# 52 matmuls of a constant by itself, at the start of an FFT and mixture-of-experts kernel

## The chip, the cores and the metric

The kernel runs on one core of one Trainium2 chip. The metric is device time in microseconds of one execution. Six names come up for the engines: PE is TensorE (matmuls), PEld its weight loads, DVE is VectorE, ACT is ScalarE, POOL is GpSimd and SP is SyncE, which issues most of the DMAs here.

## What is computed

The real part of a two-dimensional Fourier transform of each of 8 batches of 2496 x 256, and then a mixture of 8 experts with one expert for each of the 19968 rows:

```python
def _attn_ref(x):                       # x: 8 x 2496 x 256, f32
    X = np.fft.fft(x, axis=1)
    X = np.fft.fft(X, axis=2)
    return X.real.astype(np.float32)

def _moe_ref(x, modality_id, w_gate, modality_bias, w1, w2):
    logits = x @ w_gate + modality_bias[modality_id]
    e_idx = np.argmax(logits, axis=1)
    ...                                 # gate_w: softmax weight of the chosen expert
    for e in range(E):                  # 8 experts, 256 -> 1024 -> 256
        mask = e_idx == e
        h = np.maximum(x[mask] @ w1[e], 0.0)
        out[mask] = gate_w[mask, None] * (h @ w2[e])
    return out
```

## The kernel before

The transform is done batch by batch as small matrix products. Stage 1 (line 540) multiplies x by constants `c1`: for each of two halves of the 10 column groups of a batch (`c` = 0 and 1) there are four units, each with its own PSUM tile of the pool `psf`, which has four slots, and ACT copies each unit out of PSUM (line 513). In the first batches the products are in f32. For the scale of the numbers ACT also squares the input and sums it up (line 394), four times for a batch, and four small matmuls by `ones` (line 418) add the sums over the partitions. Stages 2 and 3 (lines 571 and 586) follow, then a routing step that puts each row on the list of its expert (GpSimd scatters the rows to DRAM), and blocks of 256 rows that run through the two products of their expert (lines 1099 and 1119). These blocks take most of PE's time, and the transform of later batches runs between them.

The expert weights arrive in f32 and are split into two f16 parts each. `wload` (line 827) loads 1024 KB into a tile `wa`; `wfold` (lines 835 and 836) adds and subtracts its two halves on DVE; `wnorm` (line 849) takes the norm by matmuls of the weights by themselves into a tile of the PSUM pool `psm`, which has three slots; then follow the split (lines 870 and 877) and the store to DRAM.

At the beginning SP issues the loads in this order: a part of x, half of `c1`, further parts of x, the other half of `c1`, the packed constants and small tables. Then `ones` is set by a memset on DVE (line 293). All DMAs of SP go down one queue.

The order of the instructions on each engine is not that of the program: the framework plans it with modelled times (`schedule_with_timeline_sim=True`, line 1313), by what is ready and by place in the program, and each engine then runs its list in that order. Where the kernel says `issue_after` or `high_priority`, it bends that plan.

Of the kernel before, what the change touches and what calls it, by code (L numbers as in the profile page):

```python
# [13 lines left out]
F32 = mybir.dt.float32  # L14
# [8 lines left out]
P = 128  # L23
# [48 lines left out]
ORDER0 = "rrrrrrrfssssFssss"  # L72
PACK = 1000 + 512
UB = 3
RV = 1
FG = 6
ORDER_S = (0, 1, 2), (0, 1, 2, 3, 3, 4, 4, 5, 5, 6, 6, 7, 7), (5, 6, 7, 0, 1, 2, 3, 4)
# [121 lines left out]
class Group:  # L199


    def __init__(self, k, b, g0, rp, tail, dsti):
        self.k, self.b, self.g0, self.gn = k, b, g0, min(CH, G - g0)
        self.rp, self.tail, self.dsti, self.list, self.first = rp, tail, dsti, None, False
# [28 lines left out]
class Pads:  # L233

    b, list = B - 1, None
# [8 lines left out]
class Kernel:  # L244
    def __init__(self, ctx, tc, t):
        self.ctx, self.tc, self.nc, self.t = ctx, tc, tc.nc, t
        nc = self.nc
        pool = lambda name, bufs=1, **k: ctx.enter_context(tc.tile_pool(name=name, bufs=bufs, **k))
        self.cpool = c = pool("consts")
        self.fft = pool("fft", 2)  # L250
        self.rt = pool("route", 2)
        self.psf = pool("psf", 4, space=PSUM)
        self.psm = pool("psm", 3, space=PSUM)
        self.pso = pool("pso", 1, space=PSUM)
        self.pool = pool

        self.ready = -1
        self.early = True
        self.head = None
        self.XM = [None, None]  # L260

        def const(name, shape, dt=F32):
            x = c.tile(shape, dt, name=name)
            nc.sync.dma_start(x, t["c_" + name])
            return x

        self.load_x(0, 0, 0)
        self.c1 = c.tile([P, NI, 132], F32, name="c1")
        nc.sync.dma_start(self.c1[:, 0:NH], t["c_c1"][:, 0:NH])
        self.load_x(0, 0, 1)  # L270
        if XE:
            self.load_x(0, 1, 0)
            nc.sync.dma_start(self.c1[:, NH:NI], t["c_c1"][:, NH:NI])
            self.load_x(0, 1, 1)
            pk = const("pack", [P, PACK])
        else:
            pk = const("pack", [P, PACK])
            self.load_x(0, 1, 0)
            nc.sync.dma_start(self.c1[:, NH:NI], t["c_c1"][:, NH:NI])
            self.load_x(0, 1, 1)  # L280
        self.mp = pk[:, 0:512].rearrange("p (a c) -> p a c", a=4)
        self.misc = pk[:, 512:584]
        self.pk = pk
        self.wg = pk[:, 584:616].rearrange("p (a c) -> p a c", a=4)
        self.e3 = pk[0:120, 616:616 + 2 * P].rearrange("p (a c) -> p a c", a=2)
        self.iota = pk[0:1, 872:1000]
        self.ids = const("ids", [P, B, NC], I32)
        self.tri = const("tri", [P, 2, P], F16)
        self.mb = c.tile([P, 2, 8], F32, name="mb")
        nc.sync.dma_start(self.mb, t["mb"].unsqueeze(0).to_broadcast([P, 2, 8]))  # L290

        self.ones = c.tile([P, P], BF16, name="ones")
        nc.vector.memset(self.ones, 1.0)
        self.base = c.tile([P, 8], F32, name="base")
        nc.vector.tensor_copy(self.base, self.misc[:, 16:24])
        pad = c.tile([P, ROW], I16, name="padrow")
        nc.gpsimd.memset(pad, 0)
        padi = pad.bitcast(I32)
        nc.gpsimd.memset(padi[:, 256:257], OOB)
        self.padrow = pad  # L300
        for i in range(2):
            self.scatter_dep(nc.sync.dma_start(t["xd"][DUMP + i * P: DUMP + (i + 1) * P, :], pad), 0)
        self.done = c.tile([1, 8], F32, name="done0")
        nc.vector.memset(self.done, 0.0)
        self.ntok = 0
        self.extra = 0
        self.ntaken = 0
        self.nblk = 0
        self.loads = []
        self.pend = []  # L310
        self.rows = None
        self.nslot = NSLOT
        self.prev = None
        self.ob = None
        self.off = 0
        self.mark = None
        self.bases = {}
        self.pos = 0.0
        self.paced = None, 0, 1
        self.slots = lambda b: 1  # L320
        self.hold = ()
# [65 lines left out]
    def fold_add(self, b, c):  # L387
        n = 4 if b < UB else 2
        if c == 0:
            self.sq = self.fft.tile([P, n], F32, name=f"nst{n}")  # L390
        if b < UB:
            jk = self.wp.tile([P, NH * D], F16, name="xj", bufs=1)
            for h in range(2):
                self.nc.scalar.activation(jk.rearrange("p (i d) -> p i d", i=NH), self.XM[c][:, h], AF.Square, accum_out=self.sq[:, 2 * c + h:2 * c + h + 1])
            return
        X = self.XM[c][:, 0]
        for i0, i1 in PARTS:
            self.nc.vector.tensor_tensor(X[:, i0:i1], X[:, i0:i1], self.XM[c][:, 1, i0:i1], ALU.add)
        self.nc.scalar.activation(self.XM[c][:, 1], X, AF.Square, accum_out=self.sq[:, c:c + 1])
# [56 lines left out]
    def scale(self, b):  # L456
# [6 lines left out]
        inv = rt.tile([P, 1], F32, name="xinv")  # L463
        self.pow2(self.total(self.sq, self.psf.tile([P, 512], F32, name="psf")), eb, s, 204 if b >= FB else 188, 2.0 if b < UB else 1.0)
        V.tensor_scalar(inv.bitcast(I32), eb.bitcast(I32), float(66 << 23), None, ALU.add)
# [7 lines left out]
    def fold(self, b, c):  # L473
# [7 lines left out]
        elif c == 0:  # L481
            self.fold_add(b, 0)
            self.fold_add(b, 1)
            self.scale(b)
        if b < UB:
            self.PQ = self.XM[c][:, :, :, 0:P], self.XM[c][:, :, :, P:D]
# [33 lines left out]
    def stage1(self, b, c):  # L520
# [3 lines left out]
        for h, src in enumerate(self.PQ):  # L524
# [3 lines left out]
            for i0, n in ((0, 3), (3, 2)):  # L528
# [4 lines left out]
                for i in range(n):  # L533
                    o = v[:, :, 12 * i:12 * i + 12]
                    if b >= FB:
                        for k, (a, w) in enumerate(HL):
                            nc.tensor.matmul(o, src[:, a, i0 + i, :], self.c1h[:, w, i1 + i, :], start=k == 0, stop=k == 2)  # L537
                    elif b < UB:
                        for k in range(2):
# [5 lines left out]
                else:  # L545
                    self.copy(T1[:, :, cols], v, b < UB and (h + i0 // 3) % 2 < E1)
                yield
# [775 lines left out]
```

## Time and profile before

| | us |
|---|---|
| median of three timed runs | 1032.98 |
| lowest and highest of them | 1031.93, 1036.22 |
| the profiled execution | 1029.87 |
| its span, first to last instruction | 1028.0 |
| PE busy in the span | 999.3 |
| DVE, ACT, POOL busy | 542.7, 443.3, 368.7 |

The profile is of one execution, and its rows give the time from the span's start. Matmuls are pipelined: one begins before the one ahead of it has ended, so the distance of two starts is the price of one, and the duration is longer. The idle time of an engine is put down to what released it. A row of the timeline in which equal instructions are merged gives the first start, the time from there to the last end, and how many there are.

### The profile page before, as it was taken

How to read it: one execution, taken by the hardware profiler on the slowest of the kernel's cores; microseconds unless marked ns; L12 is line 12 of the kernel's file. 1: busy time of each engine (PE TensorE's matmuls, PEld its weight loads, DVE VectorE, ACT ScalarE, POOL GpSimd, SP SyncE). 2: the span in 40 equal slices, each digit the busy share in tenths (PEclk: the TensorE clock that was granted, in tenths of full speed). 3: DMA queues.
4: the chain of work that ended last, by engine and by line, in shares of the span. 5: the costliest groups of instructions: out<-in, count | busy, mean ns of one | idle time of the engine just before them, and what ended most of it. 6: DMA issues, size and time to landing. Idle time of an engine off the chain costs nothing.

```text
span 1028.0 us, 25873 instructions
## 1 busy us (share of the span) xinstructions
PE 999.3 (97%) x9910; PEld 904.1 (88%) x9910; DVE 542.7 (53%) x1607; ACT 443.3 (43%) x870; POOL 368.7 (36%) x351
## 2 busy tenths in 40 slices
PE   7999899999999999999999999999999999999996
PEld 6878789898998899999999998888888888899996
DVE  2869767586866558779763347423232322222221
ACT  4775676466643354455533333233332323233332
POOL 0077822136414432735343334345451212121111
PEclk9999999999999999999999999999999999999999
DMA  9847969268459858988766963887788895594991
GB/s 335 328 140 234 368 165 302 73 229 255 153 153 283 310 172 240 300 258 281 229 188 199 232 184 86 268 258 238 173 241 229 259 256 176 159 289 139 235 205 36
DMA packets 149725, 227.65 MB, mean 221 GB/s; under 512 B 116309, under 2 KB 117375, under 8 KB 132695
## 3 DMA queue, kind: packets, MB, share of 16 engines
q1 hardware_dynamic: 133031, 183.75, 61.8%
q0 software_dynamic: 16560, 42.15, 11.5%
q8 instruction: 80, 1.31, 0.5%
q14 instruction: 54, 0.44, 0.1%
HBM read 191.77 MB, written 62.48 MB: 247 GB/s over the span
## 4 chain that ended last, share of the span: by engine, by line
PE 77%; issue 10%; DMA 7%; POOL 2%; DVE 2%; ACT 1%; POOLq 0%; SPq 0%; ACTq 0%
PE psm L1099 33%; PE pso L1119 33%; DMA wa<-w 4%; DMA XM<-x 2%; PE psf L540 2%; PE psf L566 2%; POOL out L1128 2%; PE psf L584 2%; PE psf L571 2%; PE psf L537 2%; PE psf L586 1%; DMA c<-c_c 0%; PE psm L849 0%; ACT w L870 0%; DMA xT<-xd 0%
## 5 line engine op out<-in xcount | busy, mean ns | idle before, releaser
L1099 PE MATMUL psm<-xT,w 128*128 128x256 f16 (+1 forms) x4368 | 453.3, 260 | 5.4 <-DVE H L1105 3.3
L1119 PE MATMUL pso<-w,H 128*128 128x256 f16 x3864 | 450.5, 273 | 2.7 <-ACT ob L1127 2.7
L1099 PEld LDWEIGHTS <-w 128*128 128x128 f16 x4368 | 383.6, 98 | 44.3 <-issue 4.3
L1119 PEld LDWEIGHTS <-H 128*128 128x128 f16 x3864 | 375.2, 98 | 45.5 <-issue 3.2
L1105 DVE SCALAR_TENSOR_TENSOR H<-psm,H 128x512 f16<-128x512 f32 x322 | 219.9, 687 | 331.9 <-ACT H L1104 331.2
L1128 POOL DMA_INDIRECT out<-ob,ig x161 | 163.6, 1016 | 514.1 <-ACT ob L1127 484.0
L1104 ACT ACTIVATE H<-psm 128x512 f16<-128x512 f32 x322 | 190.7, 596 | 224.3 <-PE psm L1099 223.1
L1127 ACT ACTIVATE ob<-pso,gs 128x256 f32<-128x256 f32 x161 | 68.6, 471 | 247.6 <-PE pso L1119 204.5
L709 POOL DMA_INDIRECT xd<-rp,dsti x88 | 102.1, 1161 | 96.4 <-DVE rm L228 49.2
L709 POOL DMA_INDIRECT xd<-rm,dsti x88 | 94.3, 1072 | 35.5 <-issue 18.3
L518 DVE SCALAR_TENSOR_TENSOR T<-psf,T 120x280 f16<-120x280 f32 (+2 forms) x95 | 43.2, 462 | 42.3 <-ACT T L517 42.2
L877 DVE SCALAR_TENSOR_TENSOR w<-wa,wsc,w 128x512 f16<-128x512 f32 (+1 forms) x52 | 42.5, 867 | 10.8 <-ACT w L870 10.8
L517 ACT ACTIVATE T<-psf 120x280 f16<-120x280 f32 (+2 forms) x95 | 38.7, 421 | 10.2 <-PE psf L537 5.7
L571 PE MATMUL psf<-m2u,T 128*120 128x280 f32 x132 | 37.2, 403 | 1.8 <-DVE Lg L594 1.0
L540 PE MATMUL psf<-c,XM 128*128 128x132 f32 x240 | 31.9, 296 | 6.8 <-DMA c<-c_c 6.8
L540 PEld LDWEIGHTS psf<-c,XM 128*128 128x128 f32 x240 | 30.8, 206 | 7.0 <-DMA XM<-x 6.7
L584 PE MATMUL psf<-T,pack 120*128 120x145 f16 x330 | 34.7, 224 | 1.4 <-DVE T L518 1.4
L870 ACT ACTIVATE w<-wa,wsc 128x1024 f16<-128x1024 f32 (+1 forms) x24 | 33.4, 1426 | 4.3 <-DVE wsc L406 3.5
L566 PE MATMUL psf<-pack,T 128*120 128x144 f16 (+1 forms) x330 | 31.3, 229 | 0.0
L513 ACT COPY T<-psf 120x280 f32<-120x280 f32 (+2 forms) x57 | 22.7, 407 | 16.6 <-PE psf L571 7.3
L856 ACT ACTIVATE xj<-wa 128x1024 f16<-128x1024 f32 x20 | 21.1, 1054 | 18.2 <-DMA wa<-w 7.4
L517 ACT ACTIVATE rp<-psf 128x256 f16<-128x256 f32 x55 | 21.0, 383 | 16.2 <-PE psf L584 12.5
(186 smaller groups left out, 596.9 us busy)
## 6 DMA issues: line engine op xcount, KB each, us to landing
w<-w SPq DMA_DIRECT2D x80, 1028.0 KB
w<-w SPq DMA_DIRECT2D x80, 1024.0 KB
XM<-x SPq DMA_DIRECT2D x14, 1280.0 KB
wa<-w SPq DMA_DIRECT2D x16, 1024.0 KB
out<-ob,ig POOLq DMA_INDIRECT x161
XM<-x SPq DMA_DIRECT2D x2, 768.0 KB
xT<-xd SPq DMA_TRANSPOSE x91
xd<-rp,dsti POOLq DMA_INDIRECT x88
```

The lines of the kernel that those rows point to most:

```text
L517: self.acted = self.nc.scalar.activation(dst[:, 0], ps, AF.Identity, scale=scale).ins
L540: self.staged = nc.tensor.matmul(o, src[:, k, i0 + i, :], self.c1[:, i1 + i, :], start=k == 0, stop=k == 1).ins
L566: nc.tensor.matmul(oh, T1[h][:, a, g, :], self.m2h[h][:, w], start=h + k == 0, stop=h * k == 2, skip_group_check=True)
L571: nc.tensor.matmul(ps[0:120, 0:280], T1[h][:, g, :], self.m2u[h], start=h == 0, stop=h == 1)
L584: nc.tensor.matmul(ps3[0:P, cols], self.e3h[:, a, j, :], T2[:, w, cols], start=k == 0, stop=k == 2)
L709: i = self.nc.gpsimd.indirect_dma_start(out=self.t["xd"], out_offset=bass.IndirectOffsetOnAxis(ap=at, axis=0), in_=row, in_offset=None, bo ...
L1099: l1 = nc.tensor.matmul(ps[:, q, :], w1v[:, h, kt, ft], xT[:, xs, :], start=k == 0, stop=k == 5).ins
L1104: nc.scalar.activation(H[:, 0, f0:f0 + NF, :], ps, AF.Relu)
L1105: self.mark = V.scalar_tensor_tensor(H[:, 1, f0:f0 + NF, :], ps, 0.0, H[:, 0, f0:f0 + NF, :], ALU.max, ALU.subtract).ins
L1119: nc.tensor.matmul(po[:, tg, :], H[:, hh, ft, tg * P:(tg + 1) * P], w2v[:, wh, ft, :], start=k == 0, stop=k == 23)
L1127: self.ob = nc.scalar.activation(ob, po[:, tg, :], AF.Identity, scale=gs[:, tg:tg + 1]).ins
L1128: ins = nc.gpsimd.indirect_dma_start(out=t["out"], out_offset=bass.IndirectOffsetOnAxis(ap=ig.bitcast(I32)[:, tg, 0:1], axis=0), in_=ob, i ...
```

## The change

Right after `ones` is set, a PSUM tile of the pool `psm` is taken, and 52 matmuls of `ones` by `ones` (128 x 128 by 128 x 128, bf16) are added up in its first 128 columns. Nothing reads the tile.

```diff
@@ constants @@
 UB = 3
+WARM = 52
 RV = 1
@@ Kernel.__init__ @@
         self.ones = c.tile([P, P], BF16, name="ones")
         nc.vector.memset(self.ones, 1.0)
+        ps = self.psm.tile([P, 2, 256], F32, name="psm").rearrange("p a b -> p (a b)")
+        for i in range(WARM):
+            nc.tensor.matmul(ps[:, 0:P], self.ones, self.ones, start=i == 0, stop=i == WARM - 1)
         self.base = c.tile([P, 8], F32, name="base")
```

## Rows read from the trace of the kernel before

**Rows 1.** Stretches: us, each engine busy (instructions), granted clock, DMA share, GB/s

```profile
0.00:20.00 20.00, 13.11 (x90) 13.03 (x91) 4.34 (x39) 10.02 (x21) 0.83 (x6) 1.00 0.88 309
20.00:82.00 62.00, 57.93 (x447) 49.72 (x447) 44.43 (x179) 45.91 (x89) 23.03 (x22) 1.00 0.64 238
82.00:800.00 718.00, 710.53 (x6897) 641.25 (x6897) 434.44 (x1281) 320.47 (x639) 302.98 (x280) 1.00 0.76 226
800.00:1028.00 228.00, 217.73 (x2483) 200.11 (x2480) 59.47 (x111) 66.86 (x123) 41.85 (x43) 0.99 0.69 194
```

**Rows 2.** Timeline of PE: start us, us, line, out<-in, shapes, count [idle before]

```profile
6.76 7.64 PE L540 MATMUL psf<-c,XM 128*128 128x132 f32 x40 [6.76 <-DMA c<-c_c]
14.23 0.19 PE L418 MATMUL psf<-nst,ones 128*128 128x1 bf16 x2
...
16.73 0.17 PE L418 MATMUL psf<-nst,ones 128*128 128x1 bf16 x1
16.76 2.50 PE L540 MATMUL psf<-c,XM 128*128 128x132 f32 x20
19.09 0.52 PE L334 MATMUL psf<-awm,pack 128*128 128x16 f32 x4
...
21.08 0.63 PE L849 MATMUL psm<-wa 128*128 128x128 bf16 x8
```

**Rows 3.** Line 540 in 7 to 12.5, then 13 to 14.2: ns min/median/max

```profile
L540 PE MATMUL psf<-c,XM x26: 424/424/557, 6.8 to 12.4; 128*128 128x132 f32 x26
...
L540 PE MATMUL psf<-c,XM x13: 276/276/277, 12.8 to 14.1; 128*128 128x132 f32 x13
```

**Rows 4.** Stretch of the slow matmuls (columns: PE, PEld, DVE, ACT, POOL, clock)

```profile
6.70:12.70 6.00, 5.94 (x27) 5.97 (x28) 0.00 (x0) 4.60 (x8) 0.00 (x0) 1.00 1.04 406
```

**Rows 5.** Timeline of DVE at the start

```profile
0.89 0.17 DVE L293 MEMSET ones<- 128x128 bf16 x1
```

**Rows 6.** Timeline of ACT, 8 to 17 us

```profile
8.06 1.28 ACT L394 ACT_TABLE_LOAD   x1 [8.06 <-DMA XM<-x]
...
15.46 0.21 ACT L394 ACTIVATION_READ_ACCUMULATOR xj<-XM 128x1 f32 x1
15.55 0.38 ACT L513 COPY T<-psf 128x264 f32<-128x264 f32 x1
...
16.93 0.38 ACT L513 COPY T<-psf 128x264 f32<-128x264 f32 x1 [0.39 <-PE psf L418]
```

**Rows 7.** Timeline of DVE, 18 to 22 us

```profile
19.42 0.17 DVE L339 COPY m2p<-psf 128x16 f32<-128x16 f32 x1 [0.93 <-PE psf L334]
...
19.81 1.22 DVE L835 TENSOR_TENSOR wa<-wa 128x1024 f32<-128x1024 f32 x1
```

**Rows 8.** Line 849 in 21 to 21.6: durations, and what it waited for

```profile
L849 PEld LDWEIGHTS <-wa x8: 96/97/100, 21.1 to 21.4; 128*128 128x128 bf16 x8
L849 PE MATMUL psm<-wa x8: 218/218/232, 21.1 to 21.5; 128*128 128x128 bf16 x8
...
  DVE wa L835: 0.3, 1
```

**Rows 9.** Timeline of SP: the first four weight loads are issued

```profile
14.10 2.09 SPq L827 DMA_DIRECT2D wa<-w  x4
```

**Rows 10.** DMA, 0 to 5.9 us: packets, MB moved, share; loads with KB

```profile
q1 hardware_dynamic: 420, 1.14, 62.6%
...
XM<-x SPq DMA_DIRECT2D x2, 768.0 KB
...
c<-c_c SPq DMA_DIRECT2D x2, 330.0 KB
```

**Rows 11.** DMA, 15.2 to 18.9 us: packets, MB moved, share

```profile
q1 hardware_dynamic: 134, 1.05, 89.3%
```

**Rows 12.** Stretch while the next weight loads move (last column: GB/s)

```profile
19.80:26.10 6.30, 6.23 (x45) 5.26 (x46) 3.42 (x9) 3.08 (x11) 0.00 (x0) 1.00 1.01 423
```

**Rows 13.** A piece of the chain that ended last: start, us, what

```profile
94.76 27.56 DMA wa<-w
```

## The prediction

> **What bounds the kernel now.** I read busy time by stretches first, then the first 22 us instruction by instruction. The four stretches add up to 999.30 us of busy TensorE (PE) in a span of 1028.0; VectorE (DVE) comes next with 542.7 [rows 1]. By stretch, PE stands idle 6.89 us in the first 20 us, 4.07 us from 20 to 82, 7.47 us from 82 to 800, and 10.27 us after that, most of it the last output on its way out [rows 1]. So a gain must come out of PE's own work or out of those idle spots, and whatever is saved early has to survive every wait that is tied to something else than PE, a transfer above all.
>
> The first thing the reader is to see is that PE's first work runs slowly. PE starts at 6.76, when the first x and the first constants have landed, and 40 matmuls of the first transform stage take until 14.23, 7.47 us. The last 20 of the same kind, same shape, take from 16.76 to 19.09, 2.33 us [rows 2]. At that pace 40 would take 4.66. The durations say where the pace changes: 424 ns each up to 12.5, 276 ns each from 13 on [rows 3]. The granted-clock column shows 1.00 over this stretch [rows 4], which does not agree with the durations; I go by those. Read so, PE ran at the lower level (1.2 GHz) from its first matmul until about 12.6, after some 5.9 us of unbroken matmuls, and at 2.4 GHz from there. The lower level costs 7.47 - 4.66 = **2.81 us of PE time**, and that is all there is to win.
>
> **What the change adds.** 52 matmuls of `ones` by `ones`, 128 columns, each with a weight load, ahead of everything else on PE: in the order of the program they come before the first transform matmul, and they need only the memset of `ones`, which ends at 0.89 + 0.17 = 1.06 [rows 5]. PE has nothing to do until 6.76. So they begin at about 1.1. Their price each is not in the trace at this place; bounds: eight bf16 matmuls of the same shape at the high level take 0.63 us with the last one's 0.22, so (0.63 - 0.22)/7 = 0.059 us apart [rows 2, 8]; the dearest near row is the slow transform matmul, 27 of which fill 7.47 - 13 x 0.117 = 5.95 us, 0.22 apart [rows 2, 3]. I take the first, slowed by the ratio of the two paces, 0.22/0.117 = 1.9: 0.11. Then 52 take 5.7 us and end at 6.8, against 6.76 when the data is there; the bounds are 4.2 and 12.5. Cover: PE's wait for the first loads; without it the whole 5.7 would be paid. One slot of three of the tile psm is taken; its next user is PE itself at 21.08 [rows 2], so no one waits for it. What is queued behind the burst is all of PE's work, and the first to wait for that is ScalarE (ACT), whose first copies out of PSUM come after two squares that no PE work touches.
>
> **What it speeds up.** The burst is as long, 5.7 us, as the run of matmuls after which the pace rose. So I take the clock to be at the high level from about 7, and the 40 matmuls to end at 6.8 + 4.7 = 11.5 instead of 14.23: 2.7 us early.
>
> **Where that goes, first wait.** PE's queue is in order. Ahead of the last 20 transform matmuls stands the last of four small sums (line 418, at 16.73), which needs the fourth square's accumulator, read by ACT at 15.46 + 0.21 = 15.67; and the next PSUM slot (psf has four) comes free with ACT's copy at 15.55 + 0.38 = 15.93 [rows 2, 6]. ACT started at 8.06 on the landing of x and has not been idle in between, so neither time moves. The last 20 begin at 16.0 instead of 16.76: of 2.7 us, 0.75 is left; the rest turns into PE waiting for ACT. They end at 18.3, and DVE copies their sequel at about 18.65 instead of 19.42 [rows 2, 7].
>
> **Second wait.** Next in PE's queue, at 21.08, stand the matmuls on the first expert weights (line 849). PE's weight load already stood idle 0.3 us there for DVE's fold of those weights, line 835 at 19.81 [rows 7, 8]. That fold needs the load wa(0), 1024 KB, issued at 14.10 [rows 9]. The queue moved 1.05 MB, just this load, from 15.2 to 18.9 [rows 11]. From last bytes to consumer there is a lag: the first x and constants, 768 + 330 KB = 1.12 MB, were moved by 5.9, and PE started on them at 6.76, 0.87 later [rows 2, 10]. 18.9 + 0.87 = 19.77. So the fold, although DVE's own work ran right up to it, could hardly have begun before 19.81, and DMAs do not start earlier by this change: their issue waits for other DMAs. With bounds for the lag of 0 and 0.9, the gain that passes this point is between 0.75 and nothing; I take 0.05. From 21 us on every queue goes on as it did.
>
> **The sum.** 5.7 us of new PE work, hidden; -2.8 us of PE time; +0.05 us from the burst's end; +1.95 waiting for ACT; +0.75 waiting for the fold's load: -0.05 us. Against the profiled execution, 1029.87 us (1.87 around the span of 1028.0), that is 1029.8. That execution lies 3.1 below the median of the three timed runs, 1032.98, and I forecast for the median: **1032.9 us, no change**.
>
> **A rule weighed.** The trace shows weight loads of 97 ns inside a spacing of 59 ns [rows 2, 8], so a load runs beside the matmul before it. The Trainium skill, "TensorE: Matmul & The Clock Gate", section "Part 3: Packing small matmuls — row/col tiling", says a weight load overlaps matmuls in flight only where the row group differs. All 52 use the whole array, so by that rule load and matmul would add up: with that page's 107 ns for each at the low clock, 213 ns a pair, the burst would end at 12.2 (an estimate from that page), and the program be about 2.4 us slower. The rows above do not agree with it.
>
> **Rivals.**
> - *Overrun (slower).* The burst's pairs cost more than 0.11, and PE is late for its data. From a burst that ends at T, PE is ready for line 849 at T + 4.66 + (19.09 - 14.23) + (21.08 - 0.3 - 19.09) = T + 11.2, and it is late only past 21.05: T over 9.85, a pair of over (9.85 - 1.1)/52 = 0.168 us. At the upper bound of 0.22, T is 12.5, PE 2.65 late, and the stage after it is dense enough (PE idle 4.07 of 62 us [rows 1]) to keep that: 1035.6. For it: the pair at the low clock is not in the trace. Against: the overlap just shown. Chance 0.07.
> - *The gain passes the second wait.* If the lag of wa(0) was shorter than I read, 0.75 us goes through to a stage where PE is the bound: 1032.2. Against: 0.87 of lag fits 19.81 to 0.04 us. Chance 0.06.
> - *It does not do what it says.* The clock is back at or still on the lower level when the data comes, and the 40 matmuls take 7.5 us again: 1033.0, the same time for another reason. Chance 0.05.
> - *Another order.* The program's order is planned with modelled times (line 1313). If in that plan the burst ends after the first data, orders change far from here. What that costs depends on transfers: at 423 GB/s a load of 1024 KB takes 2.5 us [rows 12], and the wait for a weight load at 94.76 is already 27.56 us long in the chain that ended last [rows 13]; three loads out of place there cost 7.4, about 1040. It decides if the chain's load comes behind others on the one load queue. To the other side, PE idles 4.07 + 7.47 us between 20 and 800 [rows 1]; to gain 5.2 nearly half of it must vanish, about 1027.5. Chance 0.20: 0.08 faster and 0.09 slower by over 0.5%, 0.03 in between.
>
> **How the numbers follow.** Forecast 0.62, rivals 0.07, 0.06, 0.05, 0.20. A measurement of this kernel tells some 0.5% (5.2 us) from no change, that is, below 1027.8 or above 1038.1. Within: 0.62 + 0.07 + 0.06 + 0.05 + 0.03 = 0.83; faster 0.08, slower 0.09, both from the other order. The range: the whole 2.81 us would give 1030.2, the overrun 1035.6, and the timed runs reach to 1036.22; 1030.0 to 1036.2 holds all but the other order, which leaves out under 0.2.
>
> **What would show it.** In the profile after: 52 matmuls from about 1.1 to 6.8 on PE; transform matmuls of 276 ns from about 7 instead of 424; the first 40 done near 11.5, then PE idle until about 12.5 and again before 15.7; the last 20 from 16.0; line 339 near 18.65; line 835 still at 19.8, and PE's wait ahead of line 849 grown from 0.3 to about 1 us, with the page alike from there. I am wrong if line 835 begins well before 19.7 and the lead lasts (then DVE, not the load, set it), if transform matmuls start later than 9.85, or if the order of instructions after 21 us differs.

## The result: slower by half a per cent

The changed kernel takes 1038.15 us (median of 10 runs, 1036.57 to 1041.86), the kernel before 1032.7 beside it (10 runs, 1029.70 to 1037.76). The ratio is 1.0051, 95% interval 1.0032 to 1.0071; forecast were no change and 1030.0 to 1036.2. The profiled execution after is a median one, 1038.48 us with a span of 1036.7. The profiled execution of before, 1029.87, turned out to be the second lowest of 46 times of that kernel on chips like this one (1029.70 to 1039.77), so a profile of after looks worse against it than the medians are.

The stretches after, as in [rows 1] (us, busy time of PE, PEld, DVE, ACT, POOL, granted clock, DMA share, GB/s):

```profile
0.00:20.00 20.00, 17.08 (x149) 16.32 (x150) 4.39 (x39) 11.04 (x25) 0.83 (x6) 1.00 0.89 304
20.00:82.00 62.00, 59.36 (x460) 51.17 (x459) 45.80 (x192) 45.52 (x87) 24.18 (x23) 1.00 0.64 240
82.00:800.00 718.00, 704.49 (x6787) 632.81 (x6787) 431.12 (x1262) 315.40 (x631) 288.55 (x277) 0.99 0.75 223
800.00:1036.00 236.00, 227.24 (x2570) 208.61 (x2567) 61.91 (x116) 69.57 (x128) 43.75 (x45) 0.99 0.71 197
```

TensorE (PE) is busier than before up to 82 us and 6.04 us less busy from 82 to 800, with 110 matmuls fewer done in that time. So the start went as meant, and the loss lies later. The start, PE's timeline as in [rows 2] (line numbers after are higher by 4 from here on):

```profile
1.11 5.21 PE L297 MATMUL psm<-ones 128*128 128x128 bf16 x52 [1.11 <-DVE done L308]
6.85 4.74 PE L544 MATMUL psf<-c,XM 128*128 128x132 f32 x40 [0.53 <-DMA c<-c_c]
...
12.51 0.16 PE L422 MATMUL psf<-nst,ones 128*128 128x1 bf16 x1 [0.92 <-ACT xj L398]
12.78 3.87 PE L544 MATMUL psf<-c,XM 128*128 128x132 f32 x32
...
19.71 2.15 PE L575 MATMUL psf<-m2u,T 128*120 128x280 f32 x8 [0.21 <-ACT m2u L359]
...
23.39 0.62 PE L853 MATMUL psm<-wa 128*128 128x128 bf16 x8
```

The 52 matmuls end at 6.32, inside the wait for the first data, and the first 40 transform matmuls take 4.74 us where they took 7.47. But the matmuls on the first expert weights (line 853, before: 849) now stand behind twelve of line 575 and four of line 590, not ahead of them: the planner, whose modelled times the 52 matmuls shift, wrote another order for the first 70 us or so. PE no longer waits for the fold of those weights, which starts at 20.18, and keeps a lead.

Where the lead ends. PE at the first up-projection, before and then after:

```profile
79.80 4.77 PE L540 MATMUL psf<-c,XM 128*128 128x132 f32 x40
85.03 4.09 PE L1099 MATMUL psm<-xT,w 128*128 128x256 f16 x36 [0.47 <-DMA xT<-xd]
```

```profile
85.76 6.50 PE L1103 MATMUL psm<-xT,w 128*128 128x256 f16 x35 [4.03 <-DMA xT<-xd]
```

The transpose that this work needs was not issued earlier. SyncE's queue before, then after:

```profile
81.66 1.36 SPq L1080 DMA_TRANSPOSE xT<-xd  x1
```

```profile
82.06 1.37 SPq L1084 DMA_TRANSPOSE xT<-xd  x1
```

It follows GpSimd's scatters, whose first begins at 50.65 us before and at 50.61 after. So PE is through with its own work at 81.73 and idle for 4.03 us. The granted clock then (after):

```profile
81.70:85.70 4.00, 0.03 (x1) 0.00 (x0) 3.76 (x6) 0.38 (x1) 3.23 (x3) 0.80 0.59 130
85.70:91.00 5.30, 5.24 (x25) 3.63 (x25) 5.30 (x13) 0.60 (x1) 4.24 (x4) 0.50 1.08 171
91.00:97.00 6.00, 5.94 (x39) 4.77 (x37) 5.94 (x14) 3.30 (x7) 4.78 (x5) 1.00 1.00 353
```

0.50 is the lower level (1.2 GHz): the up-projection that took 4.09 us before takes 6.50 for 35 of its 36 matmuls. A second such place lies at 353 us, where the order of instructions is the same in both kernels (before, then after):

```profile
353.21 0.47 PE L584 MATMUL psf<-T,pack 120*128 120x145 f16 x5 [1.39 <-DVE T L518]
```

```profile
356.80 0.22 PE L588 MATMUL psf<-T,pack 120*128 120x145 f16 x1 [3.23 <-ACT T L521]
358.53 0.74 PE L588 MATMUL psf<-T,pack 120*128 120x145 f16 x5 [1.51 <-DVE T L522]
```

There, too, the clock falls behind the idle time (0.50 from 358.5 to 364 us). DVE waits there for a load of x, 8.85 us where it was 5.34, which SyncE issues at 342.44 us, before at 338.40. The first reading was therefore: the new order turns the lead into one long idle spot, the clock falls, and transfers do the rest.

### The profile page after: what moved, and what is told of

Its sections match the earlier page's. It is cut to its first block, busy times and chain, and to the rows that moved or that the text cites. A ratio compares the mean times of both kernels' runs of the same rounds, so it can differ in the third digit from the quotient of the medians.

```text
span 1036.7 us, 25975 instructions
## 1 busy us (share of the span) xinstructions
PE 1008.2 (97%) x9962; PEld 908.9 (88%) x9962; DVE 543.2 (52%) x1607; ACT 441.5 (43%) x870; POOL 357.3 (34%) x351
## 3 DMA queue, kind: packets, MB, share of 16 engines
q0 software_dynamic: 16560, 42.15, 11.5%
## 4 chain that ended last, share of the span: by engine, by line
PE 71%; issue 10%; DMA 10%; DVE 3%; ACT 2%; POOL 2%; SPq 0%; POOLq 0%; DVEq 0%; ACTq 0%
PE psm L1103 31%; PE pso L1123 30%; DMA XM<-x 5%; DMA wa<-w 4%; POOL out L1132 2%; PE psf L570 2%; PE psf L588 2%; PE psf L575 2%; PE psf L541 1%; PE psf L544 1%; PE psf L590 1%; ACT xj L398 1%; DVE XM L402 0%; ACT w L874 0%; DVE H L1109 0%
## 5 line engine op out<-in xcount | busy, mean ns | idle before, releaser
L1103 PE MATMUL psm<-xT,w 128*128 128x256 f16 (+1 forms) x4368 | 458.3, 262 | 7.4 <-DMA xT<-xd 4.0
L713 POOL DMA_INDIRECT xd<-rp,dsti x88 | 93.7, 1065 | 97.9 <-DVE rm L229 49.2
L713 POOL DMA_INDIRECT xd<-rm,dsti x88 | 90.1, 1024 | 38.0 <-issue 17.4
L588 PEld LDWEIGHTS <-pack 120*128 120x128 f16 x330 | 25.4, 98 | 6.2 <-issue 5.0
L860 ACT ACTIVATE xj<-wa 128x1024 f16<-128x1024 f32 x20 | 21.1, 1053 | 21.5 <-DMA wa<-w 10.3
L544 PEld LDWEIGHTS psf<-c,XM 128*128 128x128 f32 x240 | 27.8, 190 | 2.3 <-ACT T L517 1.4
L544 PE MATMUL psf<-c,XM 128*128 128x132 f32 x240 | 28.9, 279 | 0.8 <-DMA c<-c_c 0.5
```

Of the source, the lines that this page charges most:

```text
L544: self.staged = nc.tensor.matmul(o, src[:, k, i0 + i, :], self.c1[:, i1 + i, :], start=k == 0, stop=k == 1).ins
L588: nc.tensor.matmul(ps3[0:P, cols], self.e3h[:, a, j, :], T2[:, w, cols], start=k == 0, stop=k == 2)
L713: i = self.nc.gpsimd.indirect_dma_start(out=self.t["xd"], out_offset=bass.IndirectOffsetOnAxis(ap=at, axis=0), in_=row, in_offset=None, bo ...
L1103: l1 = nc.tensor.matmul(ps[:, q, :], w1v[:, h, kt, ft], xT[:, xs, :], start=k == 0, stop=k == 5).ins
```

## Experiments

In some kernels instructions of PE are put in or taken out after the order has been made, so that the order stays as it was planned: `ones_pairs(ins)` gives the places of each load of the ones and its matmul, `clones` copies them. With 3 matmuls planned ahead, PE, ACT, DVE and GpSimd run the order of the kernel before ("old order"); with 52, that of the changed kernel ("new order"). Line numbers are those of the changed kernel, or higher by 1.

The runs fell on chips of two kinds: on some the kernel before takes 1033 to 1036 us, on others 1075 to 1077. A ratio always compares with the kernel before on the same chip. The first four runs were on one chip of the first kind, all others on three chips of the second.

**The changed kernel again** (nothing altered).

> The changed kernel once more, nothing altered: a second profile of it. It tells which of the two places where it falls behind belong to the program: the idle 4.03 us of TensorE at 81.7 us (on the transpose xT<-xd) with the granted clock at 0.5 right behind it, and the idle 3.23 + 1.51 us at 353 to 358 us (behind a load of the input 4 us late) with its own fall of the clock. Theory (both come from the program's order): both stand again, at the same places, and the time is 1037 to 1039 us. Rival (the second is an accident of the transfers in that one execution): the first stands, the second doesn't, the profiled span is 5 to 6 us shorter, near 1031 us, and the median lies between 1034 and 1038.

1.0047 (1.0030 to 1.0065). The first idle spot stands, with a lower clock behind it (0.66 from 86 to 91 us):

```profile
86.25 5.76 PE L1103 MATMUL psm<-xT,w 128*128 128x256 f16 x36 [4.20 <-DMA xT<-xd]
```

At 354 us PE is idle for 1.68 + 1.51 us, not 3.23 + 1.51: the place of the second spot stands, its size changes from one execution to the next. The loss of 0.5% is real.

**The old order with all 52.**

```diff
-WARM = 52
+WARM = 3
+    a, b = ones_pairs(ins)[1]
+    ins[b + 1:b + 1] = clones(nc, (ins[a], ins[b]), 52 - WARM)
```

> The instructions in the order of the kernel before on every engine, with all 52 matmuls of the ones ahead of them: 49 copies are put in after the order is made. Theory (the new order is what costs, the 52 matmuls by themselves do nothing): the first 40 transform matmuls run at about 276 ns and end near 11.5 us, TensorE then waits for the fold of the first weights as in the kernel before and the lead is gone by 21 us; no fall of the clock before the tail; 1032 to 1033.5 us. Rival (the 52 matmuls do harm on the chip, in whatever order, by an early full clock that is taken back later): granted clock 0.5 in stretches of some us before the tail, and 1036 to 1039 us.

1.0059 (1.0035 to 1.0083): as slow as the changed kernel, so the theory fell. The new order is not needed for the loss. The first 20 us go nearly as the forecast had them, PE waits for the fold and the lead is gone (PE, and DVE's fold):

```profile
12.60 0.19 PE L423 MATMUL psf<-nst,ones 128*128 128x1 bf16 x2 [1.06 <-ACT T L518]
...
20.61 1.23 DVE L840 TENSOR_TENSOR wa<-wa 128x1024 f32<-128x1024 f32 x1 [1.01 <-DMA wa<-w]
21.90 0.63 PE L854 MATMUL psm<-wa 128*128 128x128 bf16 x8 [1.17 <-DVE wa L840]
```

The rival's sign, a lower clock before the tail, is there once (0.62 from 112 to 116 us), but so it is in the new order with 2 matmuls (0.71). PE is 0.82 us later at the first weights than in [rows 2], for the fold starts at 20.61 where [rows 7] has 19.81. The issue of the four weight loads takes 3.13 us on SyncE's queue where it took 2.09 [rows 9], and one more transfer moves at that time. DMA queues from 14 to 17 us (packets, MB, share), old order with 52, then before:

```profile
q1 hardware_dynamic: 553, 0.63, 87.1%
q8 instruction: 1, 0.02, 2.2%
```

```profile
q1 hardware_dynamic: 503, 0.64, 84.7%
```

That packet is 16 KB of PE's code. In the trace the first fetch after the start lies at 23.6 us before, at 15.0 to 15.1 in all four profiles of this chip kind with 52 matmuls ahead (104 instructions, a load and a matmul each), and at 21.5 with two. The Trainium skill, "Runtime: NRT & Kernel Launch", section "Terms", says that an engine's instruction memory is refilled in blocks of 16 KiB; the packet sizes agree. That the packet holds up the load is not shown: on the second kind of chip, in two profiles of the kernel before, without such a packet, the fold starts at 20.25 and 20.61, and in three with 104 other instructions ahead and the packet at 15 us at 20.06, 20.36 and 21.21.

**The new order with 2 matmuls.**

```diff
+    for a, b in reversed(ones_pairs(ins)[1:-1]):
+        del ins[b], ins[a]
```

> The order of the changed kernel on every engine, but 50 of the 52 matmuls taken out after the order was made: two run. Theory (the order costs only where an early lead of 2.83 us becomes one idle stretch that lets the clock fall): the first 40 transform matmuls run at about 424 ns again and end near 14.2 us, so TensorE reaches the wait for xT at 81.7 us some 2.7 us later than in the changed kernel, is idle there for 1 to 1.5 us, not 4.03, and keeps its clock; the first up-projection is at most 0.5 us late against the kernel before; 1032 to 1034 us. Rival (the new order costs by itself, through the order in which the norms, folds and input loads are queued, whatever the clock does): 1036.5 to 1039 us with the stretch at 353 us as in the changed kernel.

1.0014 (0.9992 to 1.0036): the order alone costs at most 0.36%. Compared directly, the changed kernel is 2.9 us slower than this one (difference of the means of 12 executions each on the same chip, 95% interval 0.7 to 5.1). One part of the expectation was wrong all the same:

```profile
86.63 5.61 PE L1104 MATMUL psm<-xT,w 128*128 128x256 f16 x36 [4.01 <-DMA xT<-xd]
```

PE is idle for 4 us here too, without any early clock. So the idle spot comes from the new order, which leaves PE through at 82.62 (84.56 before) while the scatters begin at 51.36; the early clock makes PE 0.6 to 0.9 us earlier still, and xT 0.4 to 0.9 us earlier.

**The changed kernel with 64 more pairs in the idle spot.**

```diff
+    j = next(j for j, i in enumerate(ins) if type(i).__name__ == "InstMatmult" and "@xT256" in str(i))
+    fill(nc, ins, pair, j, 64)
```

> The changed kernel with 64 more matmuls of the ones on TensorE just ahead of the first up-projection, where it is idle for 4.03 us: at the 56 ns of a pair at the full clock they take 3.6 us. Theory (the idle stretch hurts by the fall of the clock behind it, 6.83 us at 0.5): the clock stays at 1.0 there, the first 36 up-projection matmuls take about 4.1 us, not 6.5, the offset to the kernel before after them is about 0.5 us, not 3.25; if the stretch at 353 us was a consequence of it, that goes too and the time is 1032 to 1034 us; if that stretch has its own cause, the time is 1035 to 1037. Rival (the fall of the clock costs nothing, since the loads of that stage set its end): the clock stays up and the time stays at 1037 to 1039.

```profile
86.13 4.09 PE L1104 MATMUL psm<-xT,w 128*128 128x256 f16 x36 [1.01 <-DMA xT<-xd]
```

The clock stays up and the 36 matmuls take 4.09 us again, against 6.61 and 5.76; the first down-projection is 1.09 us behind the profile of before, not 3.25 or 2.89. The time is 1.0027 (1.0006 to 1.0048). That is 2 us better than the changed kernel, as the timeline says it should be; the two intervals overlap, but compared directly the means differ by 2.6 us (0.5 to 4.6). 0.27% of loss stays, though the second spot has gone too in this profile: at 356 us PE is idle for 1.49 us, and the clock stays up.

Over all timed runs on this chip the mean granted clock was 0.9959 for the kernel before (35 runs; 12 for each other), 0.9924 for the changed one, 0.9932 for the old order with 52, 0.9928 for the new order with 2 and 0.9956 with the filled spot. So the new order and the 52 matmuls each go with a lower clock, and filling brings it back. But the clock doesn't account for all of the time: the new order with 2 has it as low as the old with 52 and loses a quarter as much. An estimate from the single executions (83 on this chip): within one kernel, 0.001 less of mean clock goes with 0.9 us more of time. With that taken off, what is left of the loss is 2.1 us in the changed kernel, 3.7 in the old order with 52 and 2.3 in the filled one, but -0.5 in the new order with 2, each to about 1.6. By this, something other than falls of the clock costs 2 to 4 us where the 52 matmuls are.

**The kernel before again.** It ran twice more, on chips of the second kind: 1.0009 (0.9984 to 1.0033) and 1.0009 (0.9984 to 1.0034).

> The kernel before once more, for a second profile of it: its profiled execution of 1029.87 us lies below all the other times of it seen so far (1031.29 to 1039.77), so the offsets read against it may be too large for everything that is compared with it. If so, this profile falls behind the first one by 3 to 6 us, between 80 and 480 us, with one or two falls of the granted clock to 0.5 (3.4 us each) that the first did not have; no fetch of code (16 KB) between 14 and 20 us. If the first profile is typical, the second lies within 1 us of it at every matmul up to 480 us. Time: the same as the kernel before, ratio 1.000.

The intended comparison was not to be had, since both profiles are of the other kind of chip. What that kind does differently is plain from 64 to 85 us. Stretch of before on the first kind, then on the second (its second profile there):

```profile
64.00:85.00 21.00, 19.61 (x158) 17.38 (x157) 14.20 (x73) 16.50 (x28) 13.78 (x14) 1.00 0.29 91
```

```profile
64.00:85.00 21.00, 8.24 (x41) 6.31 (x40) 2.32 (x13) 2.47 (x5) 12.90 (x14) 0.69 0.28 88
```

All compute engines but GpSimd stand still, with the DMA engines at 28%. What they waited for there (us in total, times, longest), the first of the two profiles:

```profile
DVE rp L518 <- issue: 10.1, 2, 6.4
ACT rp L517 <- remote: 8.5, 1, 8.5
...
PE psf L586 <- issue: 6.8, 1, 6.8
```

"issue" is a wait for nothing that the profile shows. In the second profile PE's long waits there are put down to ACT (10.7 us), which stands still itself. From 60 to 76 us the trace of that chip kind has no packet of code for any engine in these two profiles, and the first kind has one for PE and one for the others. That the engines had run out of code is the reading that fits; a wait for code is not itself recorded. These places are only part of the 40 us between the kinds: PE is also busy for just 13.85 of 20 us from 140 to 160 and 42.03 of 50 from 430 to 480, which wasn't followed.

**104 instructions without the clock, and the clock with 26 instructions**, both in the old order. One-column pairs in the place of the 52 (for the wide ones the patterns are `[1, 512]` and `[[128, 128], [0, 4], [1, 128]]`, and 13 stands for 52):

```diff
+    mv = dict(outs=[copy.replace(pair[1].outs[0], ap=[[512, 128], [1, 1]], bass_ap=None)],
+              ins=[copy.replace(pair[1].ins[0], ap=[[128, 128], [1, 1]], bass_ap=None), pair[1].ins[1]])
...
+    mid = clones(nc, pair, 52 - 2, **mv)
```

> The order of the kernel before, with 52 matmuls of the ones of one column each, each with its load of the ones: the 104 instructions of the change without the columns of its matmuls. Theory F (code fetched into the weight load): the fetch of 16 KB lies near 15 us again, the fold starts at 20.2 to 20.6 us, the ratio is 1.003 to 1.008. Theory C (the early clock): the clock rises only when the transform runs, at 10 to 12.7 us, if the loads alone do not raise it, the first 40 transform matmuls take 6 us or more, and the ratio is 0.998 to 1.002. If the clock rises early all the same, the run tells only of F.

> The order of the kernel before with 52 one-column matmuls once more (104 instructions ahead, no early clock), as a reference for the others of this call. Theory F (the number of instructions ahead of the rest shifts every later fetch of TensorE's code, 16 KB for 256 instructions, against the transfers that the stages wait for): ratio 1.003 to 1.007 as the first time (1.0045). Rival N (the differences of some tenths of a per cent between these kernels are chance): 0.998 to 1.002.

> The order of the kernel before, 52 one-column matmuls with their loads ahead: the 104 instructions of the change without its early clock. Where the kernel before takes 1033 to 1036 us: theory F (the fetch of code that moves to 15.0 us, and the later ones, are what costs) 1.004 to 1.007, as the 52 of 128 columns in this order (1.0059); theory C (the early clock) 0.998 to 1.002. Where it takes 1075 us the two earlier runs gave 1.0045 and 1.0027, and a third tells little.

> The order of the kernel before, with 13 matmuls of 512 columns of the ones (4 times the same 128) in the place of 52 of 128: the same columns through TensorE and the same early full clock, but 26 instructions where there were 104. Theory F (the extra instructions bring TensorE's fetch of code of 16 KB forward from 23.6 to 15.0 us, into the load of the first weights, which lands 0.4 to 0.8 us later; the delay is carried to the scatters and grows in the stretch that waits for transfers): the fetch lies at 20 us or later, the fold of the first weights starts at 19.8 to 20.2 us, and the time is 1035 to 1037 us where the kernel before has 1035.6, ratio 0.999 to 1.002. Theory C (the early clock and the early end of the first 40 matmuls do the harm): the ratio is 1.004 to 1.008 as with the 52.

> The order of the kernel before, 13 matmuls of 512 columns ahead: the early clock with 26 instructions, no fetch of code between 14 and 20 us. Where the kernel before takes 1033 to 1036 us: theory F 0.999 to 1.002, theory C 1.004 to 1.007. Third possibility, both slow or both not: then neither the number of instructions nor the clock decides by itself.

The one-column pairs take 1.55 us in all and leave the first 40 transform matmuls at 6.82 to 7.22 us, so the clock isn't early; the fetch of code lies at 15.0 to 15.3. Three runs: 1.0045 (1.0021 to 1.0070), 1.0027 (1.0001 to 1.0053), 1.0047 (1.0019 to 1.0075), mean 1.0040. The 13 wide matmuls have the early clock (40 transform matmuls in 4.74 us) and fetch at 20.4 and 22.7: 1.0032 (1.0007 to 1.0057) and 1.0008 (0.9981 to 1.0036), mean 1.0020, between the theories. So on this kind of chip, in the old order, the 104 instructions cost something without the early clock; whether the early clock costs too is not settled by the wide ones.

One place where PE falls behind is to be seen. PE, the kernel before (second profile of it on this kind), then the one-column pairs (second run):

```profile
68.52 0.16 PE L418 MATMUL psm<-wsu,ones 128*128 128x1 bf16 x1 [2.10 <-issue]
75.67 1.30 PE L586 MATMUL psf<-T,pack 120*128 120x145 f32 x4 [5.53 <-ACT T L513]
...
102.79 4.09 PE L1099 MATMUL psm<-xT,w 128*128 128x256 f16 x36
```

```profile
78.00 0.17 PE L423 MATMUL psm<-wsu,ones 128*128 128x1 bf16 x1 [9.48 <-DVE wj L856]
83.80 1.30 PE L591 MATMUL psf<-T,pack 120*128 120x145 f32 x4 [4.12 <-ACT T L518]
...
105.09 4.09 PE L1104 MATMUL psm<-xT,w 128*128 128x256 f16 x36
```

The first up-projection starts at 102.66 and 102.79 in the kernel before, at 102.62 and 102.89 with the 13 wide ones, and at 105.15, 105.09 and 106.92 with the 104 instructions (the last one had been 1.8 us late at 60 us already). A reading that would fit is that the 104 use up part of the code at hand when fetches stop. The times of the fetches do not show it: PE's last one ahead of the standstill lies at 57 us in the kernel before and at 49 to 52 with the 104, but at 51 with the 13 wide ones too, which lose nothing here. The 2.3 to 4.3 us are of the size of the 0.4%, but they do not have to last: the second of the three profiles ends 0.8 us behind the second one of the kernel before (spans of 1074.6 and 1073.8).

**A whole fetch more, and the new order.** 128 one-column pairs are 256 instructions, 16 KB, in either order; 52 one-column pairs and 13 wide matmuls were put into the new order as well.

```diff
-    mid = clones(nc, pair, 52 - 2, **mv)
+    mid = clones(nc, pair, 128 - 2, **mv)
```

> The order of the kernel before with 128 one-column matmuls, each with its load: 256 instructions, one whole fetch of 16 KB more. Theory F, by position: the fetches from 40 us on fall where they fall in the kernel before (46, 57, 74, 89, 107 us, each within 2 us), and the ratio is 0.998 to 1.002. Theory F, by number (each instruction more costs): 1.008 to 1.014, since 104 gave 1.0045. Rival N: 0.998 to 1.002 too, but then the 52 of the same call give that as well.

> The order of the changed kernel with 128 one-column matmuls (256 instructions). Theory F, by position: the fetches fall as with two matmuls (42, 56, 73, 94 us, each within 3 us), and the ratio is 0.999 to 1.003. By number: 1.009 or more. Rival (the new order itself costs, and the runs with few instructions in it were chance): 1.004 to 1.007.

> The order of the changed kernel with 52 one-column matmuls (104 instructions, no early clock). The 52 of 128 columns in this order gave 1.0051 and 1.0047, two gave 1.0014, 13 of 512 columns gave 0.9994. Theory F: 1.003 to 1.007, the number of instructions decides, not the clock. Theory C (the early clock): 1.000 to 1.003.

> The order of the changed kernel, with 13 matmuls of 512 columns in the place of its 52 of 128. Theory F: no fetch of code inside 14 to 20 us; what is left is the new order alone, which with two matmuls gave 1.0014 (0.9992 to 1.0036): ratio 1.000 to 1.003. Theory C: as the changed kernel, 1.004 to 1.007. In both the idle of 3.5 to 4.5 us on xT<-xd at 82 us stands, since it did with two matmuls.

> The order of the changed kernel with 13 matmuls of 512 columns: its early clock and its order with 26 instructions in the place of 104. Where the kernel before takes 1033 to 1036 us: theory F 1.000 to 1.003 (two matmuls in this order gave 1.0014), theory C 1.004 to 1.007 (as the changed kernel, 1.0047 and 1.0051). TensorE's idle on xT<-xd at 82 us is 3.5 to 4.5 us in both.

Old order with 128: 1.0023 (1.0002 to 1.0044), fetch at 58.8 and first up-projection at 103.88, between the two. More instructions do not cost more than 104 did, so "by number" is out; "by position" (what counts is where the fetches fall) fits its timeline but not clearly its time. New order: 128 pairs 1.0006 (0.9984 to 1.0029), 52 pairs 1.0017 (0.9997 to 1.0036), 13 wide 0.9994 (0.9968 to 1.0021) and 1.0005 (0.9977 to 1.0033). None of the four is told from no change on this kind of chip. The idle spot at 82 us that was expected of the wide ones is not there on it, for PE stands still earlier.

**The changed kernel on the second kind, and one with few instructions and the spot filled** (13 wide ahead, and 16 wide, `one`, ahead of the first up-projection).

```diff
+    ins[j - 1:j - 1] = clones(nc, (mid[0],), 1) + one
```

> The changed kernel a third time, beside the kernel before of this call. Where that takes 1033 to 1036 us: 1.004 to 1.006 as twice before. Where it takes 1075 to 1077 us (the changed kernel has not run there): theory F (104 instructions move the fetches of code) 1.003 to 1.006, since the 52 one-column matmuls gave 1.0045, 1.0027 and 1.0047 in the old order and 1.0017 in the new; if the loss is bound to the early clock as well, above all of these; if the loss belongs to the idle on xT<-xd at 82 us, which is not there on those chips, 0.999 to 1.002.

> The order of the changed kernel with 13 matmuls of 512 columns ahead, and 16 more of 512 columns (3.4 us at the full clock) where TensorE is idle on xT<-xd at 82 us: 43 instructions in all where the change has 104. Where the kernel before takes 1033 to 1036 us: if code and the fall of the clock at 84 us are the two costs, both are gone, 0.997 to 1.001; if not, 1.002 to 1.005, as the kernel with 64 more pairs (1.0027). Where it takes 1075 us: 0.999 to 1.002, as the 13 without the rest (0.9994, 1.0005).

The changed kernel is level there: 1.0004 (0.9978 to 1.0030), with its first up-projection at 101.24, before the kernel before. The other gives 1.0027 (0.9999 to 1.0055), worse than hoped. On this kind PE isn't idle ahead of the first up-projection, and the 16 matmuls take 3.62 us there from 101.22. No version beat the kernel before.

**What follows, and what stays open.** On the first kind of chip the change costs 0.5%. There the new order alone costs 0.14% at the middle of its interval, and the 52 matmuls alone, in the old order, 0.59%: it is mostly the 52 matmuls, not the order, that the loss hangs on, though the early clock was gained as meant. Filling the idle spot gives some 2 us back. That 104 instructions cost something without any early clock is shown in time (three runs) on the second kind only, and only in the old order: with the new order neither the 52 one-column pairs nor the changed kernel itself is told from no change there. That they cost it by their code is argued, not shown. On the first kind no engine stands still in that way at 64 to 85 us, and whether code or the early clock makes the loss there is open, since the one-column and the wide variants never ran there. The wide one with the clock and few instructions would tell it.

Nor is it traced to a cause where the old order with 52 loses its 6 us. Matmul by matmul against the profile of before, it is 0.8 to 0.9 us late from 22 to 105 us, 5.3 at 354 and 8.1 at 420, so the loss comes after 105 us. PE's waits from 82 to 500 us add up to 12.7 us there and to 7.5 before. Most of what is added is PE waiting for DVE to take H out of the up-projection (7.5 us against 3.3). The longest such wait ends at 111.72 us (2.85 us); DVE is late there because it has stood 4.54 us for a weight load (3.69 before). Both profiles are poor witnesses, though: this one is 4 us faster than its kernel's median, with a mean clock of 0.996 where the 12 executions have 0.9932, and the only one of before on that kind is 3 to 6 us faster than its own (1032.7 and 1035.58 on two chips).

## Why the prediction was wrong, point by point

- *2.8 us to win at the start, the burst hidden*: right. 52 matmuls from 1.11 to 6.32 (forecast 1.1 to 6.8), 0.10 us each (0.11); the 40 end near 11.5 (11.5). The row held against the rule on weight loads was right: a pair took 100 ns, not 213.
- *First wait, for ACT*: right in the old order with 52 (1.06 us idle at 12.60, the last 20 from 16.05 against 16.0). In the changed kernel ACT's copies stand ahead of squares, so the last transform matmuls end at 17.66, not 18.3.
- *Second wait, the fold of the first weights*: right in the old order with 52, where PE is idle for it 1.17 us (about 1 forecast) and DVE itself waits 1.01 us for the load. That the size fits is partly luck: PE was through at 20.73 us where the forecast has about 20.0, and the fold began at 20.61, not 19.8. In the changed kernel it fell away, because line 853 moved.
- *"From 21 us on every queue goes on as it did"*: this step failed. In the changed kernel it was the rival "another order", given 0.20, 0.09 of it slower, and the sign that the prediction named for being wrong, another order, came true. But its mechanism was not the one priced there: SyncE issues the same loads in the same order up to 420 us, so none came behind others on the load queue. PE ran ahead into a wait for xT that nothing made shorter, and the clock fell behind it: 4.03 us idle, and 6.50 us for 35 matmuls where 36 had taken 4.09.
- *The sum would have been wrong with the order kept, too.* The old order with all 52 loses 0.59% where the sum gave -0.05 us. So the same step fails without a new order: what goes on after 21 us was put at nothing, and it cost 6 us. What the sum lacked is a term for what 104 more instructions in PE's stream, or a clock that rises 7 us earlier, do later on. The runs show a cost of the first on one kind of chip (0.27 to 0.47%), and leave open which of the two it is on the kind that the forecast was for.
- *Judging the sum against the median, not the profiled execution*: right; the profiled one lay at the edge of the spread.

## What to carry to other kernels

Work that only warms an engine is not free because the engine is idle: it is code to be fetched (the first fetch moved from 23.6 to 15.0 us), and to a planner it is time, so hold the planned order fixed when it is tried. A lead counts only as far as the next wait that doesn't move with it; ask of that wait how long the engine will stand there and what its clock does after. And take a second profile of the kernel before, beside its spread, ahead of reading differences of a few us.

## What the runs showed of the hardware

- A burst of pairs of one column goes by in 1.55 us for 52, 0.03 us each, loads included, and does not raise the clock early; 13 matmuls of 512 columns (4.81 to 5.73 us) do.
- The granted clock fell behind idle times of TensorE of 4.0 to 4.2 us at 82 us each time (three profiles), and stayed up when 64 pairs left 1.01 us of idle time. It also fell behind shorter ones, of 2.2 to 2.9 us near 110 us (three profiles), and not behind 1.68 and 1.20 us at that place.
- PE's code comes in packets of 16 KB, about 1 us each on a DMA engine (2.2% of 16 engines in 3 us), while the data moves.
- On some chips the same kernel takes 1075 us, not 1033: a part of it is that from 64 to 85 us three engines stand nearly still at once, with PE busy for 8.24 us where it is 19.61 on the others, while GpSimd scatters.
